# A batch's pooled q and k summed on TensorE, and two chains of adding transfers that take turns, in an attention and two-MLP kernel

## The chip, the cores and the metric

The kernel runs on one core of a Trainium2 chip. A core has five engines with their own instruction queues: TensorE (PE in the profile; its weight loads are PEld), VectorE (DVE), ScalarE (ACT), GpSimd (POOL) and SyncE (SP), and 16 DMA engines that all queues share. The metric is device microseconds (us) of one execution of the whole program.

## The reference

Three stages follow one another. Everything is float32.

```
B, H, S, D = 4, 8, 576, 64;  factor = 4;  Sd = S // 4 = 144
q_d, k_d, v_d = mean of q, k, v over groups of 4 positions
out_up    = repeat(softmax(q_d k_d^T / sqrt(D)) v_d, 4)        # "global", 144 x 144 per head
out_local = softmax(where(|i - j| < 4, q k^T / sqrt(D), -1e9)) v   # "local" band
x = (out_up + out_local) as [2304 tokens, 512]
h = x @ w_in;  x = (h * cos(h)) @ w_out        # first MLP, d_ff 2048
h = x @ w_in2; out = (relu(h) ** 2) @ w_out2   # second MLP, d_ff 2048
```

## The kernel before

**Tiling and order.** The program has one stream for each engine, written out ahead of time. A planner (class `Plan`) takes every operation with an engine, a cost, the tiles that it reads and writes and a priority number out of the table `PRIORITIES`; it simulates the engines with these costs and writes the operations out in the order that it arrives at. On the chip each engine runs its stream strictly in that order, and waits at an instruction until its tiles are ready. Where the planner believes that TensorE would be idle before the first matmul of the output side of the MLP, it writes "fills": 128x128 bf16 matmuls of zeros into a bank that nobody reads (`busy`, L1475).

**Attention.** It runs by batch (0 to 3). A batch has 4 global units (one for 2 heads: scores 96x432, softmax, transposes, values) and 5 local units d = 0 to 4 (116 or 112 tokens each: scores of a band, softmax, transposes L892, values L913). Softmax subtracts the maximum, takes exp, sums, inverts (L734) and multiplies by the inverse, the norm (L737). For the first `EXP_SUM` local units ScalarE subtracts, exponentiates and sums at once, one instruction for each 64 columns (L721); for the others VectorE subtracts (L709), ScalarE takes one exp (L715) and VectorE sums (L729).

**Pooled operands.** Batch 0's pooled q and k (`qn_sb`, `kd_sb`) are summed by VectorE out of the local units' loads (`f_pool`, L673), its pooled v by TensorE out of four loads (`sums`, L621; `w` in the rows is the memory of the first weights, lent to these loads). Batches 1 to 3 have them summed by the transfers themselves: GpSimd issues for each of k, q and v one plain DMA and three that add in memory (L645), each waiting for the one before it. Ahead of them stands a copy of one element (`gate`, L637) that waits for a point of the MLP. The local loads qkv, and all other transfers, are issued by SP.

**MLP.** Weights come as 64-bit words; VectorE packs them into float32 (L545, L552, L557), ScalarE and VectorE split each into a high and a low part (L523, L526), and each product is three matmuls (L946 to L948). The first MLP's tokens go in rounds of 512, 384, 448, 448 and 512 columns. Round 0 converts all weights as it goes and writes the second matrix out (`w_dram`) for the later rounds. Batch 1's attention is laid between the matmuls of round 0, and batches 2 and 3 between those of the later rounds. The second MLP (from L1314) works on blocks of 768 tokens.

Of the kernel before, what the change touches and what calls it, by code (L numbers as in the profile page):

```python
# [18 lines left out]
PR = H // 2  # L19
# [13 lines left out]
EXP_SUM = 4  # L33
HOMES = ((0, 4),)
S_PE = 0.57
PV_PE = 0.51
E_ACT = ((0, 0), (0, 1))
# [265 lines left out]
class Plan:  # L303
# [5 lines left out]
    SWITCH = {"": (0.0, 0.09, 0.2), "wide": (0.0, 0.0, 0.17), "tiled": (0.095, 0.15, 0.0)}  # L309
    MODES = ("", "wide", "tiled")  # L310

    IN_TURN = ("rawi", "rawo", "w2", "p", "pt", "qkv", "t", "w1")

    def __init__(self, bufs):
        self.bufs = bufs
# [151 lines left out]
def dve(n):  # L467
    return 0.084 + 0.00104 * n
# [1133 lines left out]
```

## Time and profile before

| | |
|---|---|
| median of 3 runs | 897.72 us (893.59 to 898.08) |
| the profiled execution: own time, span of the trace | 897.3 us, 895.2 us |
| PE busy | 880.0 us, 98% of the span |
| DVE busy | 629.8 us, 70% |
| ACT busy | 384.4 us, 43% |
| POOL busy | 32.1 us, 4% |
| DMA | 201.52 MB, mean 225 GB/s |
| first matmul of the MLP | 51.87 us into the span |

Busy time counts all work of an engine, PE's fills of zeros too, so that a busy PE is not yet a useful one. The span is the trace's, from first to last instruction; the execution's own time is 2.1 us longer.

### The profile page before, as it was taken

What the parts mean: (1) busy time and instruction counts of PE and PEld (TensorE: products, weight loads), DVE (VectorE), ACT (ScalarE), POOL (GpSimd) and SP (SyncE); (2) the same over time, 40 slices, a digit from 0 to 9 for tenths busy, and PEclk for the clock granted to TensorE, in tenths of its full rate; (3) what the DMA queues carried; (4) which work ended last, traced back from release to release, by engine and by line L of the source; (5) the groups of instructions that cost most, each with busy time, mean ns of one, the idle gap of its engine ahead of it and who ended that gap; (6) DMA issues with size and microseconds to landing.
All of it is one profiled execution on the core that took longest, in us unless ns stands there. A gap on an engine that the chain in (4) does not pass through costs nothing.

```text
span 895.2 us, 15969 instructions
## 1 busy us (share of the span) xinstructions
PE 880.0 (98%) x6143; PEld 788.0 (88%) x6143; DVE 629.8 (70%) x1232; ACT 384.4 (43%) x825; POOL 32.1 (4%) x43
## 2 busy tenths in 40 slices
PE   8899999999999999999999999999999999999998
PEld 7688877899899889998888899999999999999997
DVE  6899999646753668778798799879845545464553
ACT  5755567548653665545555443223411112211111
POOL 0002110111011000000000000000000000000000
PEclk9999999999999999999999999999999999999999
DMA  9938986876577626787796789777765647664652
GB/s 299 324 118 266 256 234 226 267 199 162 175 189 185 197 72 226 244 297 262 279 334 233 287 301 320 252 244 259 253 228 174 195 153 221 224 209 158 200 184 97
DMA packets 72938, 201.52 MB, mean 225 GB/s; under 512 B 8224, under 2 KB 11552, under 8 KB 72864
## 3 DMA queue, kind: packets, MB, share of 16 engines
q1 hardware_dynamic: 68640, 189.89, 62.6%
q0 software_dynamic: 4224, 10.62, 6.6%
q8 instruction: 49, 0.80, 0.4%
q14 instruction: 25, 0.20, 0.1%
HBM read 159.58 MB, written 40.89 MB: 224 GB/s over the span
## 4 chain that ended last, share of the span: by engine, by line
PE 81%; issue 9%; DMA 7%; DVE 2%; ACT 1%; POOL 0%; SPq 0%; ACTq 0%; POOLq 0%
PE acc L946 11%; PE acc L948 11%; PE acc L947 11%; PE pp L946 7%; PE pp L948 7%; PE pp L947 7%; PE ps L946 6%; PE ps L947 6%; PE ps L948 6%; DMA qn_sb<-in_qp_dram 3%; PE acx L1395 3%; PE acx L1394 3%; PE acx L1393 3%; DMA kd_sb<-in_kp_dram 2%; DMA qkv<-in_qkv_dram 1%
## 5 line engine op out<-in xcount | busy, mean ns | idle before, releaser
L946 PE MATMUL acc<-gh,w 128*128 128x512 f32 (+2 forms) x320 | 121.9, 381 | 0.4 <-ACT w L523 0.3
L948 PE MATMUL acc<-gh,w 128*128 128x512 f32 (+2 forms) x320 | 118.6, 371 | 0.7 <-DVE w L526 0.7
L946 PE MATMUL ps<-xh,w 128*128 128x512 f32 (+2 forms) x320 | 119.0, 372 | 0.2 <-DVE xr L924 0.2
L947 PE MATMUL ps<-xl,w 128*128 128x512 f32 (+2 forms) x320 | 118.4, 370 | 0.4 <-DVE xl L526 0.4
L947 PE MATMUL acc<-gl,w 128*128 128x512 f32 (+2 forms) x320 | 118.2, 369 | 0.0
L948 PE MATMUL ps<-xh,w 128*128 128x512 f32 (+2 forms) x320 | 118.1, 369 | 0.0
L1358 ACT ACTIVATE xh<-c 128x384 fp32r<-128x384 f32 x64 | 33.6, 525 | 153.8 <-DVE c L1350 135.6
L1314 DVE TENSOR_TENSOR c<-ua,pp 128x384 f32<-128x384 f32 x96 | 52.6, 550 | 52.4 <-PE pp L948 45.3
L978 DVE SCALAR_TENSOR_TENSOR t<-ki,ps 128x512 f32<-128x512 int32 (+2 forms) x80 | 49.2, 629 | 50.0 <-ACT ki L974 49.6
L974 ACT ACTIVATE ki<-ps 128x512 int32<-128x512 f32 (+2 forms) x80 | 44.2, 552 | 85.1 <-PE ps L948 83.8
L1314 DVE TENSOR_TENSOR ua<-ua,pp 128x384 f32<-128x384 f32 x72 | 39.6, 550 | 51.3 <-PE pp L948 50.5
L948 PEld LDWEIGHTS acc<-gh,w 128*128 128x128 f32 x320 | 60.1, 188 | 9.2 <-DVE w L526 2.0
L946 PEld LDWEIGHTS acc<-gh,w 128*128 128x128 f32 x320 | 60.1, 188 | 8.5 <-ACT w L523 1.0
L946 PEld LDWEIGHTS ps<-xh,w 128*128 128x128 f32 x320 | 60.1, 188 | 8.4 <-DVE t L986 0.8
L947 PEld LDWEIGHTS ps<-xl,w 128*128 128x128 f32 x320 | 60.1, 188 | 8.2 <-DVE xl L526 1.3
L948 PEld LDWEIGHTS ps<-xh,w 128*128 128x128 f32 x320 | 60.1, 188 | 7.0
L947 PEld LDWEIGHTS acc<-gl,w 128*128 128x128 f32 x320 | 60.2, 188 | 5.9
L983 ACT ACTIVATE t<-t,halfpi 128x512 f32<-128x512 f32 (+2 forms) x80 | 52.7, 679 | 26.9 <-DVE t L978 26.3
L526 DVE TENSOR_TENSOR gl<-t,gh 128x512 fp32r<-128x512 f32 (+2 forms) x80 | 49.9, 634 | 16.7 <-ACT gh L523 15.8
L986 DVE TENSOR_TENSOR t<-t,ps 128x512 f32<-128x512 f32 (+2 forms) x80 | 49.4, 630 | 13.3 <-ACT t L983 13.0
L523 ACT ACTIVATE gh<-t 128x512 fp32r<-128x512 f32 (+2 forms) x80 | 46.0, 585 | 26.4 <-DVE t L986 13.2
L1350 DVE SCALAR_TENSOR_TENSOR c<-c 128x384 f32<-128x384 f32 x96 | 53.0, 555 | 2.1
(190 smaller groups left out, 1999.6 us busy)
## 6 DMA issues: line engine op xcount, KB each, us to landing
w<-w_dram SPq DMA_DIRECT2D x96, 512.0 KB, 4.0
gh<-w_dram SPq DMA_DIRECT2D x77, 256.0 KB, 3.4
gl<-w_dram SPq DMA_DIRECT2D x77, 256.0 KB, 3.0
rawi<-in_wi_dram SPq DMA_DIRECT2D x32, 512.0 KB, 5.4
rawo<-in_wo_dram SPq DMA_DIRECT2D x32, 512.0 KB, 5.1
w_dram<-w SPq DMA_DIRECT2D x32, 512.0 KB, 3.9
w_dram<-rawo SPq DMA_DIRECT2D x24, 512.0 KB, 3.5
qkv<-in_qkv_dram SPq DMA_DIRECT2D x15, 732.0 KB, 8.1
```

What stands on the lines that cost most here:

```text
L523: nc.scalar.activation(out=hi(), in_=src(), func=AF.Copy)
L526: nc.vector.tensor_tensor(out=lo(), in0=src(), in1=hi().bitcast(F32), op=OP.subtract)
L946: nc.tensor.matmul(ps, w_hi, r_hi, start=first, stop=False)
L947: nc.tensor.matmul(ps, w_hi, r_lo, start=False, stop=False)
L948: nc.tensor.matmul(ps, w_lo, r_hi, start=False, stop=last)
L974: nc.scalar.activation(out=tt(ki), in_=tt(hp), func=AF.Copy, scale=1.0 / TWO_PI, bias=0.25)
L978: nc.vector.scalar_tensor_tensor(out=tt(t), in0=tt(ki), scalar=-TWO_PI, in1=tt(hp), op0=OP.mult, op1=OP.add)
L983: nc.scalar.activation(out=tt(t), in_=tt(t), func=AF.Sin, bias=halfpi[:, 0:1])
L986: nc.vector.tensor_tensor(out=tt(t), in0=tt(t), in1=tt(hp), op=OP.mult)
L1314: nc.vector.tensor_tensor(out=out(), in0=a(), in1=ps(), op=OP.subtract if sub else OP.add)
L1350: nc.vector.scalar_tensor_tensor(out=x(), in0=x(), scalar=0.0, in1=x(), op0=OP.max, op1=OP.mult)
L1358: nc.scalar.activation(out=gpart(0, R, f)[:, cols], in_=x(), func=AF.Copy)
```

## The change

It has these parts.

- `EXP_SUM` names two local units, (0, 0) and (0, 1), where it counted four.
- Batch 0's pooled q and k: the ten VectorE reductions go. For each d eight float32 matmuls with the identity add every fourth column into a PSUM bank (`f_sum`, L688, 116 or 112 columns each, 40 in all), and ScalarE copies the bank into the new joint tile `qk_sb` (`f_put`, L693, 5 in all).
- Batch 0's global scores go to the accumulators' banks (`GBANK`) and not to the ring of working banks.
- For batches 1 to 3 the chains of k and q are issued in turn, and v's starts after both.
- A local load is two tiles now, `qk` and `vv`, each with 4 buffers and a DMA of its own; the home of (0, 4) is loaded in one.
- Batch 1's global norm (12 ACTIVATEs, `f_norm_act`) and its copies of q (L762 before) move from VectorE to ScalarE.
- In the planner alone: SP's operations aren't placed ahead of their time, an adding chain's end is taken 0.5 us later, and the table of priorities is new, with 3785 numbers where there were 3767. With it the counted fills go from 287 to 148.

The diff, cut to its core:

```
-EXP_SUM = 4
+EXP_SUM = ((0, 0), (0, 1))
+GBANK = (3, 1, 2, 3)
...
-                    t = max(free[e], ready_at[i])
+                    t = max(free[e], ready_at[i], ops[i][2] if e == "SP" else 0.0)
...
-                    end[i] = adding + 2.0
+                    end[i] = adding + 2.5
...
-        before = ("gate", b)
-        for nm, dst, src in some:
+        for some, before in ((some[:2], [("gate", b)]), (some[2:], [("kd",), ("qn",)])):
             for r in range(4):
                 how = OP.bypass if r == 0 else OP.add
-                op(
-                    "POOL", 0.82, key, lambda dst=dst, src=src, r=r, how=how: nc.gpsimd.dma_start(
-                        out=dst, in_=src[b, r], accum_op=how), r=[("gate", b)] + ([before] if r == 0 else []),
-                    w=[(nm,), ("pool", b, nm)],
-                )
-            before = ("pool", b, nm)
+                for nm, dst, src in some:
+                    op(
+                        "POOL", 0.82, key, lambda dst=dst, src=src, r=r, how=how: nc.gpsimd.dma_start(
+                            out=dst, in_=src[b, r], accum_op=how), r=before, w=[(nm,)],
+                    )
...
+        if x[0] == "w1":
+            op("SP", 2.08, key, ld_all, w=[x, ("v", b, d)], new=[x])
+        else:
+            op("SP", 1.36, key, ld_qk, w=[x], new=[x])
+            op("SP", 0.75, key + 0.5, ld_v, w=[y, ("v", b, d)], new=[y])
...
-                nc.vector.tensor_reduce(
-                    out=dst[:, :, DT // 4 * d:DT // 4 * d + n], in_=src.rearrange("p r (g f) -> p r g f", f=4), op=OP.add, axis=AX.X
-                )
-            op("DVE", dve(PR * 4 * n), key + 0.3, f_pool, r=[x], w=[("kd" if nm == "k" else "qn", d)])
+        def f_sum():
+            ps = new(pool_ps, [128, 2, PR, DT // 4], space=PSUM)
+            for i, (lo, m, at) in enumerate(((0, DT, 0), (NQ, DT + 6, 3))):
+                src = T[x][:, lo:lo + PR * m].rearrange("p (r n) -> p r n", r=PR)
+                for a in range(4):
+                    nc.tensor.matmul(
+                        ps[:, i, :, 0:n], id_sb, src[:, :, at + a:at + 4 * n:4], start=a == 0, stop=a == 3
+                    )
+        def f_put():
+            nc.scalar.activation(
+                out=qk_sb[:, :, :, DT // 4 * d:DT // 4 * d + n], in_=T[pool_ps][:, :, :, 0:n], func=AF.Copy
+            )
+        op("PE", POOL_PE, key + 0.3, f_sum, r=[x, ("id",)], w=[pool_ps], new=[pool_ps], mode="wide")
+        op("ACT", act(232), key + 0.3, f_put, r=[pool_ps], w=[("qn", d), ("kd", d)])
...
+        def f_norm_act():
+            for i in range(g):
+                nc.scalar.activation(out=grp()[:, i, :], in_=grp()[:, i, :], func=AF.Copy, scale=small(sm)[:, i:i + 1])
...
-        op("DVE", dve(g * n), key + 0.04, f_norm, r=[sm], w=[p])
+        if u[0] == "g" and u[1] == 1:
+            op("ACT", g * act(n, 0.07), key + 0.04, f_norm_act, r=[sm], w=[p])
+        else:
+            op("DVE", dve(g * n), key + 0.04, f_norm, r=[sm], w=[p])
```

GpSimd's stream before, from the first gate on (batch 1; `kp`, `qp`, `vp` are k, q and v by groups of four positions):

```order
L637 COPY gate<-gh 1x1
L645 DMA kd_sb<-in_kp_dram 128x576 x4
L645 DMA qn_sb<-in_qp_dram 128x576 x4
L645 DMA vd_sb<-in_vp_dram 72x1024 x4
L637 COPY gate<-sm 1x1
L645 DMA kd_sb<-in_kp_dram 128x576 x4
```

The same place of the changed kernel:

```order
L644 COPY gate<-gh 1x1
L652 DMA qk_sb<-in_kp_dram 128x576
L652 DMA qk_sb<-in_qp_dram 128x576
L652 DMA qk_sb<-in_kp_dram 128x576
L652 DMA qk_sb<-in_qp_dram 128x576
...
L652 DMA vd_sb<-in_vp_dram 72x1024 x4
L644 COPY gate<-sm 1x1
```

The eight transfers of k and q alternate; each still waits for the one before it into the same half of the tile. v's four stay last.

SP's stream before, from the first loads of pooled v on (`w_117`, `w_123`, `w_129` are lent memory of the weights; `rawi`, `rawo` weights):

```order
L609 DMA w_123<-in_vp_dram 72x1024
L609 DMA w_129<-in_vp_dram 72x1024
L541 DMA rawi<-in_wi_dram 128x1024 x2
L662 DMA qkv<-in_qkv_dram 128x512 x2
L541 DMA rawo<-in_wo_dram 128x1024 x2
L662 DMA qkv<-in_qkv_dram 128x512 x2
L662 DMA w_117<-in_qkv_dram 128x512
L609 DMA w_123<-in_vp_dram 72x1024
L609 DMA w_129<-in_vp_dram 72x1024
L541 DMA rawi<-in_wi_dram 128x1024
L662 DMA qkv<-in_qkv_dram 128x1464
```

The same place of the changed kernel (`vv` are the local values):

```order
L616 DMA w_213<-in_vp_dram 72x1024
L616 DMA w_215<-in_vp_dram 72x1024
L548 DMA rawi<-in_wi_dram 128x1024 x2
L668 DMA vv<-in_qkv_dram 128x512
L616 DMA w_215<-in_vp_dram 72x1024
L668 DMA vv<-in_qkv_dram 128x512 x3
L548 DMA rawi<-in_wi_dram 128x1024
L668 DMA vv<-in_qkv_dram 128x512
L616 DMA w_213<-in_vp_dram 72x1024
L668 DMA vv<-in_qkv_dram 128x512
```

The fourth load of pooled v (the last row but one) stands behind a fifth `vv`, which is batch 1's first and takes the buffer of batch 0's first unit. The two `rawo` have moved behind it.

ScalarE's stream before, where the second local unit ends (`pt` is a unit's transposed weights):

```order
L725 ACTIVATE sm<-sm 128x8
L898 ACTIVATE pt<-ps 128x464
L719 ACTIVATE mx<-mx 128x8
L721 ACTIVATE p,sm<-s_292,mx 128x64
L721 ACTIVATE p,sm<-s_293,mx 128x64
```

The same place of the changed kernel:

```order
L747 ACTIVATE sm<-sm 128x8
L932 ACTIVATE pt<-ps 128x464
L693 ACTIVATE qk_sb<-ps 128x8x29
L737 ACTIVATE p<-p 128x512
L693 ACTIVATE qk_sb<-ps 128x8x28
```

The third unit's nine small exponentials and sums give way to one exp (L737, with VectorE's subtraction ahead of it and sum behind it), and the copies of the sums stand between.

## Rows read from the trace of the kernel before

**Rows 1.** The page, busy time of each engine

```profile
PE 880.0 (98%) x6143; PEld 788.0 (88%) x6143; DVE 629.8 (70%) x1232; ACT 384.4 (43%) x825; POOL 32.1 (4%) x43
```

**Rows 2.** Stretches: us, busy PE, PEld, DVE, ACT, POOL, then PEclk, DMA share, GB/s

```profile
0.00:52.00 52.00, 46.60 (x744) 38.20 (x744) 40.71 (x85) 34.83 (x144) 0.20 (x4) 1.00 0.85 283
52.00:162.30 110.30, 105.95 (x789) 84.80 (x789) 104.95 (x211) 69.46 (x140) 14.39 (x16) 1.00 0.76 234
162.30:895.20 732.90, 727.44 (x4612) 665.02 (x4612) 484.16 (x938) 280.11 (x542) 17.47 (x23) 1.00 0.68 220
```

**Rows 3.** Fills of zeros (L1475) in one stretch: us, PE, PEld, as above

```profile
8.60:31.90 23.30, 12.21 (x150) 11.11 (x150) 1.00 1.02 329
```

**Rows 4.** PE's timeline, 8 to 52 us: start, us, work, [idle before <-releaser]

```profile
8.62 6.00 PE L1475 MATMUL idle<-zero 128*128 128x128 bf16 x63
...
30.00 0.77 PE L772 MATMUL ps<-kd_sb,qd_sb 128*96 128x144 f32 x5 [1.91 <-issue]
...
31.89 7.04 PE L621 MATMUL ps<-w,id_sb 72*72 72x512 f32 x16
...
48.98 3.08 PE L1475 MATMUL idle<-zero 128*128 128x128 bf16 x52
51.87 0.47 PE L946 MATMUL ps<-xh,w 128*128 128x512 f32 x1
```

**Rows 5.** DVE by form to 52 us: work, count, busy, mean, idle before

```profile
L673 DVE TENSOR_REDUCE qn_sb<-qkv 128x116 f32<-128x464 f32 x4 | 2.5, 632 | 3.1 <-DMA qkv<-in_qkv_dram 3.1
L673 DVE TENSOR_REDUCE kd_sb<-qkv 128x116 f32<-128x464 f32 x4 | 2.5, 629 | 0.0
...
L709 DVE TENSOR_TENSOR p<-s,mx 128x256 f32<-128x256 f32 x2 | 0.7, 410 | 0.0
L729 DVE TENSOR_REDUCE sm<-p 128x8 f32<-128x512 f32 x1 | 0.7, 685 | 0.2 <-ACT p L715 0.2
```

**Rows 6.** DVE by form, 52 to 162.3 us (round 0)

```profile
L737 DVE TENSOR_TENSOR p<-p,sm 96x432 f32<-96x432 f32 x4 | 2.4, 605 | 0.1
...
L762 DVE COPY qd_sb<-qn_sb 64x576 f32<-64x576 f32 x2 | 0.9, 454 | 0.8 <-DMA qn_sb<-in_qp_dram 0.8
```

**Rows 7.** ACT's timeline in the opening

```profile
15.99 0.56 ACT L898 ACTIVATE pt<-ps 128x464 f32<-128x464 f32 x1 [3.52 <-PE ps L892]
```

**Rows 8.** DMA issues to 60 us: transfer, count, KB each, us to landing

```profile
w_dram<-w SPq DMA_DIRECT2D x3, 512.0 KB, 4.7
...
qkv<-in_qkv_dram SPq DMA_DIRECT2D x4, 256.0 KB, 9.0
```

**Rows 9.** A stretch late in round 0, columns as in the second group

```profile
130.00:140.00 10.00, 9.42 (x84) 7.19 (x83) 9.85 (x19) 8.97 (x23) 1.10 (x2) 1.00 0.81 209
```

**Rows 10.** POOL's timeline, batch 1's chains

```profile
73.56 2.66 POOL L637 COPY gate<-gh 1x1 f32<-1x1 f32 x1 [73.11 <-ACT gh L523]
76.16 0.74 POOL L645 DMA_DIRECT2D kd_sb<-in_kp_dram  x1
...
93.56 0.86 POOL L645 DMA_DIRECT2D kd_sb<-in_kp_dram  x1 [5.79 <-DMA kd_sb<-in_kp_dram]
94.09 0.90 POOL L645 DMA_DIRECT2D qn_sb<-in_qp_dram  x1
102.47 0.86 POOL L645 DMA_DIRECT2D qn_sb<-in_qp_dram  x1 [7.47 <-DMA qn_sb<-in_qp_dram]
...
116.71 0.95 POOL L645 DMA_DIRECT2D vd_sb<-in_vp_dram  x1
122.47 0.83 POOL L645 DMA_DIRECT2D vd_sb<-in_vp_dram  x1 [4.81 <-DMA vd_sb<-in_vp_dram]
```

**Rows 11.** PE's timeline at batch 1's first global scores

```profile
121.38 1.71 PE L772 MATMUL ps<-kd_sb,qd_sb 128*96 128x144 f32 x12 [0.34 <-DVE qd_sb L762]
```

**Rows 12.** SP's timeline at the end

```profile
888.80 1.44 SPq L1424 DMA_DIRECT2D out_dram<-e  x2
...
891.81 0.34 SPq L1411 DMA_DIRECT2D out_dram<-rawi  x1
```

More of the change, by code (lines that the diff above doesn't have):

```diff
@@ L36 @@
 PV_PE = 0.51
+POOL_PE = 1.65
 E_ACT = ((0, 0), (0, 1))
@@ L310 @@
     MODES = ("", "wide", "tiled")
-    IN_TURN = ("rawi", "rawo", "w2", "p", "pt", "qkv", "t", "w1")
+    IN_TURN = ("rawi", "rawo", "w2", "p", "pt", "qk", "vv", "t", "w1")
     def __init__(self, bufs):
@@ L479, in body @@
     BUFS = {
-        "qkv": 4, "rawi": 2, "rawo": 2, "wm": 1, "wa": 2, "w2": 3, "p": 3, "pt": 2, "t": 2, "ki": 2,
+        "qk": 4, "vv": 4, "rawi": 2, "rawo": 2, "wm": 1, "wa": 2, "w2": 3, "p": 3, "pt": 2, "t": 2, "ki": 2,
         "mx": 4, "sm": 4, "gh": 3, "gl": 3, "e": 2, "acc": 1, "ps": 4, "w1": PAIRS,
     }
-    ATT = ("qkv", "p", "pt", "mx", "sm")
+    ATT = ("qk", "vv", "p", "pt", "mx", "sm")
     const = ctx.enter_context(tc.tile_pool(name="const", bufs=1))
@@ L502, in body @@
     xr = const.tile([128, KD, BIG], F32, name="xr")
-    qn_sb = att.tile([128, PR, SD], F32, name="qn_sb")
+    qk_sb = att.tile([128, 2, PR, SD], F32, name="qk_sb")
+    qn_sb, kd_sb = qk_sb[:, 0], qk_sb[:, 1]
     qd_sb = att.tile([128, PR, 3, 2, 48], F32, name="qd_sb")
-    kd_sb = att.tile([128, PR, SD], F32, name="kd_sb")
     vd_sb = att.tile([SD // 2, 2, DM], F32, name="vd_sb")
@@ L651, in body @@
     NQ, NK, NV = PR * DT, PR * (DT + 6), 2 * PR * D
     def local(b, d):
-        return ("qkv", b, d) if (b, d) not in HOMES else ("w1", "qkv", d)
+        return ("qk", b, d) if (b, d) not in HOMES else ("w1", "qkv", d)
     def load_local(b, d, key):
-        x = local(b, d)
-        def ld(lo, hi):
-            if lo == 0:
-                new(x, [128, NQ + NK + NV if x[0] == "qkv" else 2048])
-            nc.sync.dma_start(out=T[x][:, lo:hi], in_=qkv[b, d, :, lo:hi])
+        x, y = local(b, d), ("vv", b, d)
@@ new lines, in ld_qk, with ld_v, ld_all @@
+        def ld_qk():
+            nc.sync.dma_start(out=new(x, [128, NQ + NK]), in_=qkv[b, d, :, 0:NQ + NK])
+        def ld_v():
+            nc.sync.dma_start(out=new(y, [128, NV]), in_=qkv[b, d, :, NQ + NK:NQ + NK + NV])
+        def ld_all():
+            nc.sync.dma_start(out=new(x, [128, 2048])[:, 0:NQ + NK + NV], in_=qkv[b, d])
+        if x[0] == "w1":
[3 more added lines that the diff above has]
+            op("SP", 0.75, key + 0.5, ld_v, w=[y, ("v", b, d)], new=[y])
@@ L664, in load_local @@
         if b:
-            op("SP", 2.08, key, lambda: ld(0, NQ + NK + NV), w=[x, ("v", b, d)], new=[x])
             return
-        op("SP", 1.36, key, lambda: ld(0, NQ + NK), w=[x], new=[x])
-        op("SP", 0.75, key + 0.5, lambda: ld(NQ + NK, NQ + NK + NV), r=[x], w=[("v", b, d)])
         n = min(DT, S - DT * d) // 4
-        for nm, dst, lo, m in (("q", qn_sb, 0, DT), ("k", kd_sb, NQ, DT + 6)):
-            def f_pool(dst=dst, lo=lo, m=m, at=3 if nm == "k" else 0):
-                src = T[x][:, lo:lo + PR * m].rearrange("p (r n) -> p r n", r=PR)[:, :, at:at + 4 * n]
-                nc.vector.tensor_reduce(
-                    out=dst[:, :, DT // 4 * d:DT // 4 * d + n], in_=src.rearrange("p r (g f) -> p r g f", f=4), op=OP.add, axis=AX.X
-                )
-            op("DVE", dve(PR * 4 * n), key + 0.3, f_pool, r=[x], w=[("kd" if nm == "k" else "qn", d)])
+        pool_ps = ("ps", "qk", d)
@@ L679, in operands_of @@
+        op("PE", POOL_PE, key + 0.3, f_sum, r=[x, ("id",)], w=[pool_ps], new=[pool_ps], mode="wide")
+        op("ACT", act(232), key + 0.3, f_put, r=[pool_ps], w=[("qn", d), ("kd", d)])
     def operands_of(b, d):
         t = T[local(b, d)]
-        return (
-            t[:, 0:NQ].rearrange("p (r n) -> p r n", r=PR), t[:, NQ:NQ + NK].rearrange("p (r n) -> p r n", r=PR),
-            t[:, NQ + NK:NQ + NK + NV].rearrange("p (t r n) -> p t r n", t=2, r=PR),
-        )
+        return t[:, 0:NQ].rearrange("p (r n) -> p r n", r=PR), t[:, NQ:NQ + NK].rearrange("p (r n) -> p r n", r=PR)
@@ L686, in softmax, with values_of @@
+    def values_of(b, d):
+        v = T[local(b, d)][:, NQ + NK:NQ + NK + NV] if (b, d) in HOMES else T["vv", b, d]
+        return v.rearrange("p (t r n) -> p t r n", t=2, r=PR)
     def softmax(u, key, banks, p, views, np_, g, n, scale, on_act):
@@ L754, in unit_g @@
         s, p, pt = ("ps", "s") + u, ("p",) + u, ("pt",) + u
+        bank = s if b else ("accb", GBANK[c])
         some = [(nm, d) for d in range(ND) for nm in ("qn", "kd")] if b == 0 else [("qn",), ("kd",)]
@@ L760, in f_q @@
                     dst, src = qd_sb[pp, :, :, hh, :], qn_sb[pp].rearrange("p a (t i) -> p a t i", i=48)
-                    if b:
+                    if b > 1:
                         nc.vector.tensor_copy(out=dst, in_=src)
@@ L764, in f_q @@
                         nc.scalar.activation(out=dst, in_=src, func=AF.Copy)
-            op("DVE" if b else "ACT", 0.8 if b else 1.15, key, f_q, r=[x for x in some if x[0] == "qn"], w=[("qd",)])
+            op("DVE" if b > 1 else "ACT", 0.8 if b > 1 else 1.15, key, f_q, r=[x for x in some if x[0] == "qn"], w=[("qd",)])
         def f_s():
-            ps = new(s, [96, 3, SD], space=PSUM)
+            if b:
+                new(s, [96, 3, SD], space=PSUM)
+            else:
+                T[s] = psum.tile([96, 3, SD], F32, tag=f"acc{GBANK[c]}", name=f"sg{c}", bufs=1)
+            ps = T[s]
             new(p, [128, 512])
@@ L774, in f_s @@
                 )
-        op("PE", 0.73, key, f_s, r=[("qd",)] + [x for x in some if x[0] == "kd"], w=[s], new=[s, p], mode="wide")
-        softmax(u, key, [s], p, [lambda: T[s]], 96, 3, SD, 1.0 / 128.0, True)
+        op("PE", 0.73, key, f_s, r=[("qd",)] + [x for x in some if x[0] == "kd"], w=[bank], new=[s, p] if b else [p], mode="wide")
+        softmax(u, key, [bank], p, [lambda: T[s]], 96, 3, SD, 1.0 / 128.0, True)
         for kh in range(2):
@@ L858, in f_s @@
         def f_s():
-            q, k, _ = operands_of(b, d)
+            q, k = operands_of(b, d)
             for hh in range(2):
@@ L905, in f_pv @@
         def f_pv():
-            v = operands_of(b, d)[2]
+            v = values_of(b, d)
             for hh in range(2):
@@ L916, in f_pv @@
                             )
-        op("PE", PV_PE, key + 0.2, f_pv, r=[x, ("v", b, d), pt], w=pv + xtok(b * S + s0, n), new=pv, mode="tiled")
+        op("PE", PV_PE, key + 0.2, f_pv, r=[x if x[0] == "w1" else ("vv", b, d), ("v", b, d), pt], w=pv + xtok(b * S + s0, n), new=pv, mode="tiled")
         for o, c, m in ring(b * S + s0, n):
@@ L1465, in emit_units @@
                 load_local(u[1], u[2], key - 15.0 if u[1] else -200.0 + u[2])
-                unit_l(u[1], u[2], key, u[1] * ND + u[2] < EXP_SUM)
+                unit_l(u[1], u[2], key, (u[1], u[2]) in EXP_SUM)
     def setup():
```

497 rows, old and new, of the table PRIORITIES are left out of this document.

## The prediction

> **What bounds the kernel now.** I read the page first: PE is busy for 880.0 of 895.2 us [rows 1]. Busy isn't useful, so I asked the windows of the span for three stretches: up to the MLP's first matmul, round 0, and the rest [rows 2]. In the rest PE lacks 732.90 − 727.44 = 5.5 us of being full, and the change leaves its matmuls there as they are, but for batches 2 and 3's loads and chains. In round 0 (52 to 162.3 us) PE lacks 4.35 us while DVE is busy 104.95 of 110.30 us: there DVE bounds, and PE waits for it here and there. Late in the round DVE is at 9.85 of 10 us and PE at 9.42 [rows 9]. In the opening PE looks full, but by zeros: 150 fills between 8.6 and 31.9 us fill 12.21 us [rows 3], and more run until 51.87 us [rows 4], while the DMA engines are at 1.02 of their share and DVE is 40.71 us busy of 52. What can be won lies ahead of 51.87 us and in round 0's 4.35 us; every microsecond later than that is worth itself, since PE is dense behind it.
>
> **The opening.** In PE's order a fixed chain of work leads to the sums of v (31.89 us) and from there to the MLP's first matmul, 51.87 − 31.89 = 19.98 us later [rows 4].
>
> *Ahead of the sums of v.* The fills written there go from 150 to 32. By their 12.21 us of busy time, less what overlaps (the last 52 take 51.87 − 48.98 = 2.89 us at a pitch of 56 ns, though the row says 3.08), 150 are some 11.5 us and 32 some 2.5: −9.0 us. The waits there fall as well, since the pooled operands no longer pass through DVE: the longest was 1.91 us [rows 4], and with two smaller ones I take −2.4. Some other matmuls change side of this point (one group of transposes and one of scores fewer, one group of values more): −0.5.
>
> Against that come the 40 sums of q and k. The nearest row is the same work, the sums of v: 16 records of 512 columns in 7.04 us, 0.44 us each, two records to an fp32 matmul [rows 4]. 40 matmuls are 80 records of 116 columns: 80 × 0.44 × 116/512 = 8.0 us. The first are slower: the first 63 fills take 6.00 us, 95 ns each, where the last 52 take 56 [rows 4]; the granted clock says 1.00 for the whole stretch [rows 3], so that I go by the pitches. The first 8 to 10 sums stand where these fills stood, so I add 1.9 us: +9.9. Columns read with a stride of four were in no row of PE; I take them as no dearer, and up to twice (+8) as the upper bound. Sum ahead of v: −9.0 − 2.4 − 0.5 + 9.9 = −2.0, and by the positions of the last local units −2.9 at best; I take −2.5: the sums of v start at 29.4 us.
>
> *From there on* 22 fewer fills are written (108 to 86), 1.2 us, and the groups that changed side cost 0.6: 19.98 − 0.6 = 19.4. The MLP starts at 48.8 us, **−3.1 us**. What must hold for it: weights converted in time (DVE is relieved, below), and the fourth load of v. It now stands on SP behind batch 1's first `vv`, which waits for the buffer of batch 0's first unit, free when that unit's values are done, about 23.4 us by my sum. Issued near 24.2, it lands at 28.9 if it takes 4.7 us, the row of transfers in an unsaturated stretch, and at 33.2 if it takes the 9.0 us that the local values took in the saturated one [rows 8]. By then the new order has issued less (both `rawo` stand behind it), so I go by the first; the second makes the opening's gain nothing.
>
> *ScalarE's copies of the sums* stand ahead of the second unit's exponentials, so ACT now waits there for PE. ACT was idle 3.52 us before 15.99 us [rows 7], which covers it. Five copies of 232 columns come, and two units of eight small exps with their reads become one exp each; ACT is 34.83 us busy of 52 [rows 2]. At nothing, and at most the 2 us by which the copies would hold up the second unit if that cover were gone.
>
> **DVE.** Ten reductions go at 0.63 us: −6.3. Two local units change to the form with VectorE's subtraction and sum: 2 × (2 × 0.41 + 0.69 + 0.15) = +3.3 [rows 5]. In round 0 batch 1's norms go (4 × 0.605) and its copies of q (2 × 0.454): −3.3 [rows 6]. Together −6.3 of some 146 us to 162.3; by pitch I count 5.7. It is spent first on the earlier start (3.1), what is left (2.6) on round 0's stalls. Since PE's lack there is 4.35 us, and part of the waits at the round's end are for ACT, I take **−2.0**, bounds 0 and −4. ACT takes over 12 norms and two copies; with 69.46 of 110.30 us busy it has room, though in 130 to 140 us it is at 8.97 of 10 [rows 9], which is why −4 isn't the value. These places are spread over more of the round now (batch 1's units start earlier in PE's order).
>
> **The two chains.** Before, the twelve transfers run one behind the other but for two places: q's first is issued 0.53 us behind k's last (93.56, 94.09), v's first right behind q's last. Alone, k's first three links take 93.56 − 76.16 = 17.4 us, 5.8 each. The two links with company take 102.47 − 94.09 = 8.4 and 122.47 − 116.71 = 5.8 us, 7.1 at the mean [rows 10]. So a pair costs about 1.3 us more than one, not twice as much; a round with its second issue is 7.1 to 7.6. The gate waits for the same product of the MLP. Its 73.56 would become 70.5 with the MLP's start, and may come up to 1.5 earlier where DVE, which works ahead of that product, has less in its queue; with its own 2.66 the first issue is at 71.5 to 73 [rows 10]. The last pair follows three rounds later, at 93.5 to 95, q's last lands some 4.5 us behind its issue (before, the scores ran at 121.38 [rows 11], 4.7 us behind v's first, which is right behind q's last), and ACT's copy of q takes 1 us more: 99 to 101. PE comes to the scores, now 222 matmuls into the MLP where they were at 300, at 48.8 + 222 × 0.232 = 100.2 (300 matmuls went from 51.87 to 121.38). They are on an edge: I put **+0.5** in the sum, between 0 (rounds of 6.5 us) and +4 (rounds of 8.4, the dearer pair), since PE runs in order and each 0.5 us a round costs it 1.5.
>
> [...]
>
> **Tail.** The order of the last outputs has changed: at the end stand now a VectorE copy and a store of two blocks, where the last was a store of one. The double stores are 1.44 us for two, 0.72 each, the single one 0.34 [rows 12]: +0.4, and the copy's difference makes it **+0.5**.
>
> **Sum.** −3.1 − 2.0 + 0.5 + 0.5 = −4.1 against the profiled execution's own 897.3 us: 893.2. That execution lies 0.4 below the median of the runs shown: **893.6**.
>
> **Rivals.**
>
> *A, slower: the chains don't run beside each other.* Eight links at 5.8 us from 72 are 46 us: the scores could run near 118 instead of 100, with PE waiting some 18 us at one place, and ACT too, which has the copies of q at the head of its stream. Some is given back, as DVE converts on meanwhile: about +13 in place of −4.1, so 907 to 911. It decides from rounds of 8.4 us, where +4 eats the gain; at 10 us the kernel is slower. For it: the first pair took those 8.4 us. Against it: the second pair, and a DMA share of 0.76 and not 1. Chance 0.10.
>
> *B, no change: the opening gives nothing.* The sums of q and k are dearer than the row of v's (a stride of four, or a slower clock for longer), or the fourth load of v lands at 33. Then the MLP starts at 51.5 to 52, and −2.0 + 0.5 (the chains are no later than PE then) leave 896 to 896.5. For it: the load's place on SP and saturated transfers. Chance 0.17.
>
> *C: round 0's stalls all go.* DVE's relief reaches every late place: −4 in place of −2, and an opening of −4, the chains in time: −4 − 4 + 0.5 make 890.2, and 888 where the tail costs nothing and the sums run at full pace. For it: DVE is the bound for 100 us. Against: part of the waits are for ACT. Chance 0.15.
>
> *D: the order of matmuls meets new waits in rounds 1 to 4*, since batches 2 and 3 get other loads and chains: +1 to +5 on the sum, 894.5 to 898.5. Their chains have some 4 us of slack more than batch 1's by the positions. Chance 0.10; the forecast keeps 0.48.
>
> **How the numbers follow.** A change under 0.5% (4.5 us) can't be told from none. 893.2 bounds faster; the forecast lies 0.4 short of it, so somewhat under half of it (0.21), all of C (0.15) and, where an opening gains more than I took, some hundredths of D and B count as faster: 0.41. A is slower than 902.2 in most of its 0.10: 0.08. The rest, 0.51, is within 0.5%. The range from 888.0 (C's end) to 898.5 (D, and A's rounds of 8.4 us with B's opening) leaves out A's large case. The forecast's own range is 891 to 896.
>
> **What the changed kernel's profile would show.** The sums of v near 29.4 us and the MLP's first matmul near 48.8; later than 51 would be B, and the fourth load of v or the sums' duration would say which. The ten L673 rows are gone, and the 80 records of L688 take 8 to 10 us. In the chains the first issue lies near 72, the eighth below 96, and the scores run near 100 with under 2 us of idle time before them; over 4 us there, waiting for the copy of q, is A. Round 0 shows PE idle for some 2 us instead of 4.35, and ends at 157.7 us (−4.6) in place of 162.3. DVE to the end of round 0 shows about 6 us less work. The forecast is wrong most easily by the chains: by 3 us for each microsecond that a round takes more.

## The result and the profile after

The changed kernel takes 900.58 us, the median of 9 runs (899.08 to 903.59), beside 895.75 us for the kernel before in as many. The ratio is 1.0052, with a 95% interval of 1.0031 to 1.0074: slower by half a per cent, and the interval leaves out 1. I had forecast 893.6 us, and no more than 898.5.

The profiled execution's span is 898.3 us, 3.1 more than before. Its page has this line for the engines:

```profile
PE 886.9 (99%) x6084; PEld 792.9 (88%) x6084; DVE 622.3 (69%) x1224; ACT 391.9 (44%) x814; POOL 30.1 (3%) x43
```

The windows in the three stretches of [rows 2] (up to the MLP's first matmul, round 0, the rest):

```profile
0.00:53.30 53.30, 51.56 (x684) 43.02 (x685) 36.36 (x80) 32.03 (x115) 0.20 (x4) 1.00 0.76 248
53.30:164.40 111.10, 107.15 (x797) 85.07 (x794) 106.50 (x214) 75.74 (x156) 13.74 (x19) 1.00 0.79 248
164.40:898.30 733.90, 728.16 (x4611) 664.80 (x4608) 479.44 (x932) 284.17 (x545) 16.11 (x21) 1.00 0.66 219
```

The opening is 1.4 us longer than before, where 3.1 less were forecast; round 0 is 0.6 longer, the rest 1.0. (By the windows round 0 seems 0.8 longer, 111.1 beside 110.3; the window of before starts 0.13 us behind its first matmul.) In the opening PE is busier by 5 us (51.56, 46.60 before) though half the fills are gone, and VectorE is 4.4 us less busy. So PE got more work than the fills that it gave up. PE's timeline has it, with the lines that answer to [rows 4]:

```profile
7.84 6.89 PE L688 MATMUL ps<-qk,id_sb 128*128 128x116 f32 x32
...
16.39 3.43 PE L688 MATMUL ps<-w,id_sb 128*128 128x112 f32 x16
...
20.92 6.83 PE L688 MATMUL ps<-qk,id_sb 128*128 128x116 f32 x32
...
33.98 2.32 PE L628 MATMUL ps<-w,id_sb 72*72 72x512 f32 x5
...
53.31 0.48 PE L980 MATMUL ps<-xh,w 128*128 128x512 f32 x1
```

The 80 records of the sums take 6.89 + 3.43 + 6.83 = 17.15 us, 0.21 us each, the last as slow as the first. I had taken 0.10 us, and 9.9 in all. The sums of v began at 33.98 us, where 29.4 was forecast and 31.89 was before. The view of the line L688 by engine (count, then nanoseconds minimum/median/maximum, first and last start, form) shows two candidates for the price:

```profile
L688 PEld LDWEIGHTS ps<-qk,id_sb x64: 186/208/209, 7.8 to 27.2; 128*128 128x128 f32 x64
L688 PE MATMUL ps<-qk,id_sb x64: 366/387/452, 7.8 to 27.4; 128*128 128x116 f32 x64
```

Each record has a weight load of 208 ns, just the pace of the sums; and each reads every fourth column. The experiments tell the two apart.

GpSimd's timeline answers to [rows 10]:

```profile
74.11 0.36 POOL L644 COPY gate<-gh 1x1 f32<-1x1 f32 x1 [73.66 <-ACT gh L530]
74.41 0.74 POOL L652 DMA_DIRECT2D qk_sb<-in_kp_dram  x1
75.13 0.58 POOL L652 DMA_DIRECT2D qk_sb<-in_qp_dram  x1
...
95.25 0.86 POOL L652 DMA_DIRECT2D qk_sb<-in_qp_dram  x1 [3.31 <-DMA qk_sb<-in_qp_dram]
```

The chains do run beside each other: eight issues in 95.25 − 74.41 = 20.8 us, against 40.0 for the same eight before (76.16 to 116.17). The last of those eight, in the kernel before:

```profile
116.17 0.92 POOL L645 DMA_DIRECT2D qn_sb<-in_qp_dram  x1 [7.41 <-DMA qn_sb<-in_qp_dram]
```

Batch 1's scores follow without any wait of PE:

```profile
104.54 1.71 PE L806 MATMUL ps<-qk_sb,qd_sb 128*96 128x144 f32 x12
```

Compared at the same matmul of the MLP, the changed kernel is 1.45 us behind at the first, 2.08 at the end of round 0, 3.84 at the end of the first MLP, 3.37 at the last matmul; its tail is 0.26 shorter. That is 1.45 + 1.92 − 0.26 = 3.1.

### The profile page after: what moved, and what is told of

The parts are those of the page before. It is cut to its first block, busy times and chain, and to the rows that moved or that the text cites. A ratio compares the mean times of both kernels' runs of the same rounds, so it can differ in the third digit from the quotient of the medians.

```text
span 898.3 us, 15791 instructions
## 1 busy us (share of the span) xinstructions
PE 886.9 (99%) x6084; PEld 792.9 (88%) x6084; DVE 622.3 (69%) x1224; ACT 391.9 (44%) x814; POOL 30.1 (3%) x43
## 4 chain that ended last, share of the span: by engine, by line
PE 90%; DVE 5%; ACT 2%; DMA 2%; issue 0%; SPq 0%; DVEq 0%
PE acc L980 12%; PE acc L982 11%; PE acc L981 11%; PE ps L980 7%; PE ps L981 7%; PE ps L982 7%; PE pp L980 7%; PE pp L982 7%; PE pp L981 7%; PE acx L1429 3%; PE acx L1428 3%; PE acx L1427 3%; PE ps L688 2%; DMA w<-w_dram 1%; DVE w L533 1%; PE ps L947 1%
```

## The experiments

All kernels but the last keep the changed kernel's written order; only what an operation issues was replaced. "First matmul" is the start of the MLP's first matmul in the profile. The medians are of 12 runs, of 9 for the changed kernel, of 6 for "k's chain, then q's" and the last row, and of one for the steps. Each ratio is to the kernel before as it ran beside that kernel; its medians there lay between 895.75 and 897.62 us.

| kernel | median us | ratio to before (95%) | span | first matmul |
|---|---|---|---|---|
| before, its profiled execution | | | 895.2 | 51.87 |
| changed | 900.58 | 1.0052 (1.0031 to 1.0074) | 898.3 | 53.31 |
| sums of columns side by side | 892.54 | 0.9956 (0.9940 to 0.9972) | 890.9 | 45.33 |
| VectorE's reductions again | 895.50 | 0.9983 (0.9960 to 1.0006) | 894.0 | 49.50 |
| sums in pairs | 893.06 | 0.9958 (0.9939 to 0.9977) | 891.1 | 47.12 |
| k's chain, then q's | 933.60 | 1.0425 (1.0396 to 1.0453) | 931.7 | 53.75 |
| pairs, norms on VectorE | 893.96 | 0.9972 (0.9954 to 0.9990) | 892.3 | 47.38 |
| pairs, half the norms on VectorE | 892.39 | 0.9959 (0.9940 to 0.9978) | 890.4 | 46.85 |
| steps of 2 and 3 columns (one run) | 894.82 | | 893.0 | 48.14 |
| before, with sums in pairs alone | 905.06 | 1.0085 (1.0055 to 1.0115) | 905.7 | 58.98 |

### Sums of columns side by side

```
-   src[:, :, at + a:at + 4 * n:4]
+   src[:, :, at + a * n:at + a * n + n]
```

> The changed kernel, but each matmul of the sums reads its 116 or 112 columns side by side and not every fourth one (so other columns are added up than the pooling wants; the number of instructions and columns, and the written order, are the same). Theory S (the stride): the sums' records take 0.213 us in the changed kernel because of the step of 16 bytes between their columns; side by side they take 0.10 us, the sums fall from 17.1 us to about 8, the first matmul of the MLP moves from 53.3 to 46-49 us and the time from 900.6 to about 895. Rival W (the weights): each record loads the identity anew (208 ns a load) and is bound by that; the records stay at 0.21 us and the time at 900.6. Rival L (the loads): the sums get faster but something else, the fourth load of v or the weights, holds the MLP's start at 52 to 53 us.

PE's timeline of this kernel:

```profile
7.47 3.83 PE L688 MATMUL ps<-qk,id_sb 128*128 128x116 f32 x32
...
12.96 1.99 PE L688 MATMUL ps<-w,id_sb 128*128 128x112 f32 x16
...
16.05 3.73 PE L688 MATMUL ps<-qk,id_sb 128*128 128x116 f32 x32
...
45.33 0.48 PE L980 MATMUL ps<-xh,w 128*128 128x512 f32 x1
```

and its line L688:

```profile
L688 PEld LDWEIGHTS ps<-qk,id_sb x64: 186/192/193, 7.5 to 19.4; 128*128 128x128 f32 x64
L688 PE MATMUL ps<-qk,id_sb x64: 265/273/367, 7.5 to 19.5; 128*128 128x116 f32 x64
```

The same 80 records take 9.55 us; from start to start they are 112 ns apart, where the changed kernel's are 207. The weights are the same, and a load still lasts 192 ns; it lies beside the matmul before it, and can't have set the pace. Theory S holds and W falls. The MLP starts 8.0 us earlier, and the median falls by 8.0 us (the profiled span by 7.4): the sums' 7.6 us come through whole, and no load holds the start (L falls). Start and time are both lower than I expected.

### VectorE's reductions again

```
 def f_sum():
-    ps = new(pool_ps, [128, 2, PR, DT // 4], space=PSUM)
...
+    for _ in range(24):
+        busy()
 def f_put():
-    nc.scalar.activation(out=qk_sb[...], in_=T[pool_ps][...], func=AF.Copy)
+    for dst, lo, m, at in ((qn_sb, 0, DT, 0), (kd_sb, NQ, DT + 6, 3)):
+        nc.vector.tensor_reduce(...)
```

> The changed kernel in its own order, but the pooled q and k of batch 0 are reduced by VectorE again (two reductions where ScalarE's copy stood), and in the place of each group of sums on TensorE stand 24 fills of zeros (120 in all, some 6.7 us). Theory S: PE loses 17.1 us of sums and gets 6.7 of fills; VectorE gets 6.3 us back; the MLP starts at 49 to 52 us, near the 51.9 of before, and the time is 897 to 899. Rival D (what the rest of the change does in rounds 1 to 4 and in round 0 makes it slower): the start goes back, but the time stays at 900 or above.

The start is at 49.50, as expected, and the time 895.5, below what I expected. With the sums off PE the changed order has no loss against before, and no gain that the interval tells from none: what made the kernel slower are the sums, and D is not it. PE waits here for ScalarE and VectorE instead:

```profile
22.02 1.12 PE L944 MATMUL ps<-pt,vv 64*64 64x58 f32 x30 [2.00 <-ACT xr L959]
24.69 1.09 PE L923 MATMUL ps<-id_sb,p 128*128 128x128 f32 x4 [1.56 <-DVE p L760]
...
49.50 0.48 PE L977 MATMUL ps<-xh,w 128*128 128x512 f32 x1
```

### Sums in pairs

Two neighbouring columns of every four are read in one matmul, so that 2 matmuls of 232 columns take the place of 4 of 116; VectorE adds the two halves.

```
...
-   for a in range(4):
-       nc.tensor.matmul(ps[:, i, :, 0:n], id_sb, src[:, :, at + a:at + 4 * n:4], ...)
+   src = src.rearrange("p r (g a f) -> p r g a f", a=2, f=2)
+   for a in range(2):
+       nc.tensor.matmul(ps[:, i, :, 0:n], id_sb, src[:, :, :, a], start=a == 0, stop=a == 1)
...
-   nc.scalar.activation(out=qk_sb[...], in_=T[pool_ps][...], func=AF.Copy)
+   nc.vector.tensor_reduce(out=qk_sb[...], in_=T[pool_ps][:, :, :, 0:n], op=OP.add, axis=AX.X)
```

> The changed kernel in its own order, but a matmul of the sums reads pairs of neighbouring columns (two of every four, 232 columns, 2 matmuls for q and 2 for k in place of 4 and 4), so that a bank holds two partial sums for each group, and VectorE adds the two (5 reductions of 464 columns where ScalarE's copies stood). Same result as the reference. Theory S, if the pace depends on how many columns of a 16-byte step are read one behind the other: 40 records of 232 columns at 0.20 us, 8 us in all; 3.1 us more for VectorE; the MLP's start at 48 to 50 us, the time 895 to 897. If any step in the columns costs the same, records of 0.43 us and 17 us in all: the time stays at 900 to 902.

The records of 232 columns stand 204 to 212 ns apart, as long as those of 116 with the step of four: twice the columns in the same time. The first sixteen, in PE's timeline, and the MLP's first matmul:

```profile
8.22 3.58 PE L689 MATMUL ps<-qk,id_sb 128*128 128x232 f32 x16 [0.36 <-DMA id_sb<-in_ident_dram]
...
47.12 0.48 PE L979 MATMUL ps<-xh,w 128*128 128x512 f32 x1
```

They do in 3.58 us what the changed kernel's first 32 do in 6.89. This version is faster than both kernels, 893.06 us, 0.4% below before (ratio 0.9958). Its start, 47.12, and its time were below the expected 48 to 50 and 895 to 897.

### Steps of 2 and 3 columns

```
-   src[:, :, at + a:at + 4 * n:4]
+   src[:, :, at + 7 * a:at + 7 * a + 3 * n:3] if i else
+   src[:, :, 2 * n * (a // 2) + a % 2:2 * n * (a // 2) + 2 * n:2]
```

> The changed kernel, but the sums of q read every second column (a step of 8 bytes) and those of k every third (12 bytes), 116 or 112 columns each as before (so other columns are added than the pooling wants). [...] If any step is dear: both 0.21 us. If the pace goes with the step: q's near 0.14, k's near 0.18.

Eight records of q, then those of k, in the windows of L688 alone (us, busy PE and PEld with counts, clock, DMA share, GB/s):

```profile
18.10:18.99 0.89, 0.89 (x8) 0.89 (x9) 1.00 0.76 219
18.99:20.25 1.26, 1.26 (x10) 1.26 (x9) 1.00 0.79 226
```

Eight of each start in the stretch: 0.89/8 = 111 ns with a step of 8 bytes, 1.26/8 = 158 ns with 12 (the counts also hold one or two that reach in from a neighbour). With 4 bytes it was 112, with 16 bytes 207. So here a step of 8 bytes was free, one of 12 cost 46 ns a record and one of 16 cost 95. That any step is dear (0.21 us for both) falls, and so does a pace that goes with the step (0.14 and 0.18). Why the price begins between 8 and 12 bytes isn't shown.

### k's chain, then q's

```
...
+   z, r2 = divmod(2 * r + z, 4)
+   _, dst, src = some[z]
...
```

> The changed kernel in its own order, but GpSimd's eight transfers of k and q stand as before the change, k's four and then q's four. If the two chains ran beside each other (eight links in 20.8 us in the changed kernel), then in series at 5.8 us a link the last q lands near 74.4 + 8 x 5.8 = 121 us, TensorE waits some 15 us for batch 1's global scores, which stand near 104 us, and the time is 908 to 915. If the order of issue doesn't matter, it stays at 900.6.

33 us slower, more than expected, and not at batch 1 alone. PE's waits before the global scores of batches 1, 2 and 3:

```profile
110.63 0.80 PE L812 MATMUL ps<-qk_sb,qd_sb 128*96 128x144 f32 x2 [5.63 <-ACT qd_sb L800]
...
201.63 2.71 PE L812 MATMUL ps<-qk_sb,qd_sb 128*96 128x144 f32 x10 [13.03 <-DVE qd_sb L798]
...
301.16 2.21 PE L812 MATMUL ps<-qk_sb,qd_sb 128*96 128x144 f32 x8 [6.73 <-issue]
```

25.4 us stand in these three rows. The third names no releaser; that batch's eighth transfer is issued at 295.19, 6 us before the scores. Most of the rest I put down to the clock: behind each of the three waits the granted clock is 0.50. Ahead of the second and the third PE had its pace again: 0.17 us from one matmul of 384 columns to the next (188 us) and 0.20 for 448 (294 us), beside 0.23 for 512 ahead of the first (104 us), each 0.44 to 0.45 ns a column. The windows of all engines (columns as in [rows 2]):

```profile
110.60:114.50 3.90, 3.87 (x15) 3.68 (x16) 2.08 (x4) 3.67 (x6) 0.70 (x1) 0.50 0.48 80
201.60:207.00 5.40, 5.37 (x21) 5.37 (x22) 3.30 (x6) 3.50 (x10) 1.08 (x2) 0.50 0.38 55
301.10:305.00 3.90, 3.84 (x16) 3.88 (x17) 2.88 (x5) 1.97 (x4) 0.83 (x1) 0.50 0.51 75
```

The three windows are 13.2 us long. If the work in them took twice as long as at a clock of 1.00, they cost 6.6, an estimate; with the waits that is 32.0 of the span's 931.7 − 898.3 = 33.4 us.

Batch 1's wait is only 5.6, since the links there took 4.8 us (k) and 4.9 (q) at the mean, and not 5.8. GpSimd's first and eighth issue are 29.6 us apart:

```profile
74.84 0.74 POOL L658 DMA_DIRECT2D qk_sb<-in_kp_dram  x1
...
104.46 0.86 POOL L658 DMA_DIRECT2D qk_sb<-in_qp_dram  x1 [3.46 <-DMA qk_sb<-in_qp_dram]
```

My expectation had left out batches 2 and 3; the changed order puts their scores as close behind their chains. So the alternation doesn't gain its 33 us against the kernel before; it lets the scores stand earlier, and without it this order loses them.

### The norms

```
-   op("ACT", g * act(n, 0.07), key + 0.04, f_norm_act, r=[sm], w=[p])
+   op("ACT", g * act(n, 0.07), key + 0.04, f_norm, r=[sm], w=[p])
```

(in the second kernel `f_norm if u[2] < 2 else f_norm_act`; both on the version with pairs, the planner's entry left as it was)

> The version with pairs, with batch 1's four global norms on VectorE again (one instruction of some 0.6 us each in place of three on ScalarE, at the same place of the written order). Theory N (the norms hold ScalarE up): in the changed kernel TensorE waits 1.1 us for the high part of a weight that stands behind two norms on ScalarE (113 us), and 0.5 us twice soon after; these go, round 0 is 1 to 2 us shorter and the time 1 to 2 us below the version with pairs (893.1). Rival: VectorE, the bound of round 0, gets 2.4 us more; round 0 gets no shorter, and the time stays or rises by up to 2 us.

> As the one before, but only the first two of the four norms on VectorE (those ahead of the weight for which TensorE waited), the other two on ScalarE. Theory N: the waits at the first two go as well, with half of VectorE's 2.4 us: 1 to 2 us below the version with pairs. Rival: as before, no gain.

In the changed kernel PE has one long wait in round 0, for a weight of which the high part stands behind two norms on ScalarE:

```profile
114.22 0.50 PE L980 MATMUL acc<-gh,w 128*128 128x512 f32 x1 [1.14 <-ACT w L530]
```

and ScalarE at that time:

```profile
111.19 1.02 ACT L760 ACTIVATE p<-p,sm 96x144 f32<-96x144 f32 x3
112.11 0.61 ACT L530 ACTIVATE gh<-t 128x512 fp32r<-128x512 f32 x1
112.64 1.01 ACT L760 ACTIVATE p<-p,sm 96x144 f32<-96x144 f32 x3
113.55 0.61 ACT L530 ACTIVATE w<-wa 128x512 fp32r<-128x512 f32 x1
```

Theory N read this as the norms' fault. With the norms on VectorE the same place reads:

```profile
108.86 0.50 PE L981 MATMUL acc<-gh,w 128*128 128x512 f32 x1 [1.25 <-DVE w L533]
```

The wait has only passed to the other half of the same weight, which VectorE makes. N falls. All four norms back on VectorE cost 1.2 us of span against the version with pairs (the medians differ by 0.9, inside their scatter), two of them cost nothing: 892.39 us is the lowest median of all, but not told apart from the version with pairs.

### The kernel before, with the pairs alone

The sums in pairs in the place of the first reduction of each d, VectorE's two additions in that of the second, and 120 of the 150 fills left out.

```
...
-   for nm, dst, lo, m in (("q", qn_sb, 0, DT), ("k", kd_sb, NQ, DT + 6)):
...
+   for nm, f_pool in (("q", f_sum), ("k", f_put)):
...
+   if fills <= 29 or fills > 179 or fills % 5 == 0:
+       busy()
```

> The kernel before with one part alone: batch 0's pooled q and k summed in pairs on TensorE, VectorE adding the two (two reductions of half the columns in the place of each two of before), and 120 of the 150 fills ahead of the sums of v left out; everything else in the order of before. Theory S with the rest as it was measured (the rest of the change neither gains nor loses more than 2 us behind the MLP's start): the opening gains by itself what the version with pairs gained, the MLP starts at 47 to 49 us and the time is 891 to 894. Rival: the opening's gain needs the other parts (loads in another order, VectorE's norms and the other local units' sums taken off it), since VectorE or the loads of v hold the old order; the MLP starts at 50 to 52 us and the time is 895 to 898.

It is slower than before, and its first matmul is 7.1 us later. Theory S's forecast fails; the rival has the direction, but its 50 to 52 us and 895 to 898 are both passed by 7 us. PE's first sums, the first matmul, and the windows of L678 alone (columns as for L688 above):

```profile
10.03 3.43 PE L678 MATMUL ps<-qkv,id_sb 128*128 128x232 f32 x8 [5.94 <-DMA id_sb<-in_ident_dram]
...
58.98 0.47 PE L956 MATMUL ps<-xh,w 128*128 128x512 f32 x1
```

```profile
10.00:13.50 3.50, 3.43 (x8) 2.48 (x8) 0.50 1.04 243
15.00:24.00 9.00, 7.56 (x32) 5.70 (x32) 1.00 0.94 343
```

PE stands 5.94 us for the identity, which SP loads behind four local loads in this order and behind three in the changed one. The eight records that follow that idle time take 3.43 us at a granted clock of 0.50, where the next 32 take 7.56 us, 1.89 for eight, at 1.00. So the sums, dropped in where the reductions were, didn't gain here. Whether they need the changed order for it isn't shown: my crude placing, the fills left out and the lower clock are part of that loss, and aren't separated.

## Why the prediction was wrong

The step that failed is the price of the sums: "Columns read with a stride of four were in no row of PE; I take them as no dearer, and up to twice (+8) as the upper bound." The bound was the truth: 17.15 us in place of 9.9, with 207 ns a record against 112 side by side, and the kernel with this one thing undone is 8.0 us faster. I had written it down as rival B's reason, but with the other end of that rival, an MLP start of 51.5 to 52; it was 53.31. My range left my own bound out as well: 893.6 + 8 is 901.6, and the range ended at 898.5.

Point by point:

- *Sums.* Side by side they measured 9.55 us, and 9.9 were taken, but that is luck. The row of the sums of v gave 8.0, 100 ns a record where 112 were measured; the 1.9 us for a slow start made up for it, and no slow start came: the first 32 records take 3.83 us, the last 32 3.73.
- *The rest of the opening* gains more than I took. With the sums near my price the start is at 45.33 and not 48.8; which of my other terms were too small isn't settled. The fourth load of v, which I feared, held nothing: no matmul of PE waits for it in the changed kernel or in the versions with its order.
- *DVE and round 0 (−2.0).* Nothing came back. PE's idle time in the round fell by 0.4 us (3.95, 4.35 before) where I took 2, and its busy time rose by 1.2 (107.15, 105.95 before). VectorE is 106.50 of 111.10 us busy. Of the 6.3 us that I took off it to the end of round 0 some 3 are there (36.36 + 106.50 against 40.71 + 104.95), since the softmax of a local unit more, batch 1's last, has moved into the stretch. PE's named waits in round 0 sum to 3.6 us, 4.0 before; they stand at other places, above all at the weight beside batch 1's softmax (1.14). That the norms on ScalarE are worth about 1 us is what the run with norms on VectorE suggests, with the scatter as large.
- *The chains (+0.5).* The mechanism was right: rounds of 20.8/3 = 6.9 us against 7.1 to 7.6 taken, no wait. Rival A is wrong for this order, and the serial run shows what would have hung on it. The DMA share was 0.79 in round 0, 0.76 before.
- *The tail (+0.5)* measured −0.26.
- *Behind the MLP's start* the changed order loses 1.9 us to the last matmul, where I had a gain of 1.5 (−2.0 + 0.5). In the kernels with its order and faster sums that loss is 2.5 (side by side), 1.4 (reductions) and 0.9 (pairs) us. The changed kernel has waits of 0.9 us for `w_dram` loads and 0.9 for VectorE in the later rounds that before has not, but before has others: by the windows PE's idle time behind the start is 3.95 + 5.74 = 9.7 us, and 4.35 + 5.46 = 9.8 before. It is PE's busy time that is longer, 835.3 us beside 833.4 (107.15 + 728.16, 105.95 + 727.44). What lengthens it wasn't settled: one execution of each kernel was profiled, the runs of the kernel before differ by more than that (893.58 to 903.13), and no run undid the new loads or places of batches 2 and 3.

## What to carry to other kernels

Before work goes to another engine, ask in which layout that engine will read it: a matmul that picked every fourth float32 column paid nearly twice here (207 ns against 112), and pairs of neighbours (232 columns in 204 to 212 ns) gave the pace back for a small addition elsewhere. An unknown price on the path that sets the end shouldn't be set to its lower bound because the nearest row looks alike; the row's layout is part of its price. And a wait that names one engine need not be that engine's alone (1.14 us for ScalarE here became 1.25 for VectorE): undo its work, and see whether the wait moves to the next one.

## What the runs showed of the hardware

- An fp32 matmul's pace by the step of its columns, a record of 116 columns with the same weights: 112 ns (4 bytes), 111 (8), 158 (12), 207 (16).
- A weight load that lasts 192 ns for each record didn't bound records that are 112 ns apart: the loads lay beside matmuls.
- Two chains of adding transfers beside each other took 20.8 us from the first issue to the eighth, one behind the other 29.6 us. A round of two took 6.9 us; in the run with k's chain ahead of q's one link took 4.8 to 4.9 at the mean (three of k in 14.4 us, three of q in 14.7), so two links 9.7.
- Behind waits of 5.6, 13.0 and 6.7 us PE's granted clock was 0.50 in windows of 3.9, 5.4 and 3.9 us, and ahead of the second and third wait PE had its pace again. By the estimate above these waits cost 6.6 us more than their own 25.4.
